# A Fourier filter with a routed FFN on one core: x's loads spread over two queues, part of the score sums on other engines, some first-stage chunks unfolded, and a new plan

## The chip, the cores and the metric

The program runs on one core of a Trainium2 chip, in one launch. Its engines are TensorE (PE, its weight loads PEld), VectorE (DVE), ScalarE (ACT), GpSimd (POOL) and SyncE (SP). Each works through its own list of instructions in order, and they wait for each other by semaphores. DMAs are issued from an engine's queue and run beside the engines. The metric is the device time of one execution in microseconds; a kernel's time is the median of its runs.

## The reference

For each of 8 sequences of 3136 rows by 256 channels, the program filters along the rows in the frequency domain, scores each filtered row, and sends the 128 rows with the highest scores through a gated FFN:

```python
X = np.fft.rfft(x, axis=1)
y = np.fft.irfft(X * (filt_r + 1j * filt_i)[None], n=3136, axis=1)
scores = np.einsum('bsd,d->bs', y, w_gate)
out = y.copy()
for b in range(8):
    top_idx = np.argpartition(-scores[b], 128)[:128]
    xe = y[b, top_idx]
    ye = np.maximum(xe @ w1, 0.0) @ w2
    g = 1.0 / (1.0 + np.exp(-scores[b, top_idx]))
    out[b, top_idx] = xe + g[:, None] * ye
```

All of it is fp32; x and the output are 25.7 MB each.

## The kernel before, in words

The transform of length 3136 is done as 98 times 32. A row index is split as s = 1568 h + 32 a + 16 g + n, and one sequence lies in the tile X as partition 64 g + a (49 rows in the lower half, 49 in the upper), with h, n and the channel along the partition. X is single: the same tile takes the input of a sequence, then the output of an earlier one (there it is called XO), and then the next input.

**Outer stage, inwards** (`outer`, 8 chunks of 32 channels). A chunk is folded: two subtractions or additions of X's halves h (line 347, on DVE or POOL as the table FOLD says), of which one goes to a tile xh and one back into X. Then `amm` (L355) multiplies both by a constant matrix into the PSUM tile pa, of which there is one, and `tout` (L360, a transposing copy on DVE) brings it into the big tile UU.

**Inner stage** (`inner`, 7 groups of four rows of the transform, the last with one). `zmm` (L276) makes pz, ScalarE copies it to q (L280), DVE multiplies pz by one part of the filter into y (L284), GpSimd multiplies q by the other part (L287), and `vmm` (L296) adds both products in the PSUM tile pv, of which there is one. ScalarE copies pv back into UU (L300 to L306); after that DVE multiplies pv by w_gate and sums, once for each of the four rows (`gate`, L312), which gives the scores in the transform's domain. The next `vmm` waits until the last of these has read pv.

**Outer stage, outwards.** `tin` (L339) transposes 32 channels of UU, `ymm` (L401, or three products of split operands L404 to L406 where the table SPLIT says so, whose parts L391 and L395 make) multiplies by the inverse matrix, ScalarE copies the result into X (`yout`, L409). After 8 of the 16 pieces, half of the channels is stored (L424) and the same half of a later sequence is loaded (`load`, L430). In each period the outward stage of sequence t-1, the inner stage of t and the inward stage of t+1 run interleaved.

`select` finds the 128 rows of a sequence by a search over thresholds, `ffn` gathers, multiplies and scatters them. All FFNs stand near the end of the program.

**What sets the order.** Nothing is issued in program order. Every step is recorded by `op(when, engine, cost, ...)`, and a list scheduler at the end of the kernel picks, step by step, the one that its costs say can start first, with due times and leanings from the table PLAN. The lists of all five engines, SP's and ACT's DMA issues among them, are the outcome. The eight semaphores for DMAs from SP and ACT are used in turn, so a DMA that is issued waits for the one eight before it.

**Loads before the change.** Sequences 0 and 1 are loaded with all 256 channels at a time: lower and upper rows in pieces, and the 49th row of each half in DMAs of one partition. From sequence 2 on, a half of the channels (128, rows of 512 bytes) comes in eight DMAs on SP's queue: two for partitions 0 to 47, two for 64 to 111, four for the single partitions 48 and 112. Before the first load, the partitions that pad X are zeroed (`xpad`).

## Time and profile before

| what | us |
|---|---|
| median of 3 runs | 566.62 |
| lowest and highest run | 561.68, 569.27 |
| the profiled execution, by its own time | 570.88 |
| its span, first to last instruction | 569.1 |
| TensorE busy in it | 461.7 (81%) |
| VectorE busy | 412.0 (72%) |
| GpSimd busy | 308.3 (54%) |
| ScalarE busy | 287.2 (50%) |

The profiled execution is 4.3 us above the median of the runs; 1.8 us of it lie outside the span. [...] A busy time of PE counts a matmul in full while it is pipelined with others.

### The profile page before, as it was taken

The page shows a single profiled execution, that of the slowest core. Times are in us where ns is not written, and L with a number is a line of the kernel's source. Part 1 is how long each engine was busy: PE and PEld are TensorE (multiplying, and loading weights), DVE is VectorE, ACT ScalarE, POOL GpSimd, SP SyncE. Part 2 cuts the span into 40 slices and gives each one's busy share as a digit, 9 for nine tenths or more (in the row PEclk, how much of TensorE's full clock was granted, in tenths as well). Part 3 has the DMA queues.
Part 4 walks back from the last instruction along what each step waited for, and adds up shares of the span by engine and source line. Part 5 has one row for each costly group of instructions (what it writes and reads, how often), then busy time and mean ns, then how long its engine had stood idle before and what let it go on. Part 6 is the DMA issues. An engine that isn't in the chain of part 4 may idle for free.

```text
span 569.1 us, 10223 instructions
## 1 busy us (share of the span) xinstructions
PE 461.7 (81%) x3787; PEld 239.2 (42%) x3787; DVE 412.0 (72%) x1050; ACT 287.2 (50%) x573; POOL 308.3 (54%) x203
## 2 busy tenths in 40 slices
PE   4055757798889698799769889989899976999996
PEld 4001324234344243344334334423443554666986
DVE  2065357799969588489758889878899885777442
ACT  1044223056764266256727575657556744777321
POOL 2058667777648651769158549474794555300122
PEclk9555589899999699699989999989999978999989
DMA  9993921970969349861979484959923251075401
GB/s 145 207 241 71 159 32 30 126 90 19 182 115 140 46 123 117 183 82 34 163 158 132 115 114 130 130 142 136 184 25 113 73 186 63 23 218 149 133 28 38
DMA packets 97905, 65.34 MB, mean 115 GB/s; under 512 B 4536, under 2 KB 95800, under 8 KB 97208
## 3 DMA queue, kind: packets, MB, share of 16 engines
q1 hardware_dynamic: 97088, 62.59, 58.3%
q0 software_dynamic: 768, 2.10, 1.1%
q8 instruction: 30, 0.49, 0.4%
q14 instruction: 19, 0.16, 0.1%
HBM read 37.74 MB, written 26.94 MB: 114 GB/s over the span
## 4 chain that ended last, share of the span: by engine, by line
PE 37%; DVE 25%; DMA 20%; POOL 5%; SPq 5%; issue 5%; ACT 3%; POOLq 0%; DVEq 0%; ACTq 0%
DMA X<-in_x_dram 14%; PE pv L296 8%; PE pa L355 7%; DVE rj L312 7%; PE py L401 5%; SPq L430 5%; DVE t L339 4%; DVE UU L360 4%; PE pz L276 3%; DVE y L284 3%; POOL xh L347 3%; PE pv L401 2%; DMA out_dram<-X 2%; DVE xl L395 1%; PE pm L780 1%
## 5 line engine op out<-in xcount | busy, mean ns | idle before, releaser
L287 POOL TENSOR_TENSOR q<-q,fb_sb 128x1024 f32<-128x1024 f32 (+1 forms) x56 | 124.0, 2215 | 86.0 <-ACT q L280 86.0
L355 PE MATMUL pa<-xh,c_sb 49*64 49x512 f32 x256 | 96.6, 702 | 51.8 <-DMA UU<-in_cst_dram 23.5
L347 POOL TENSOR_TENSOR xh<-X 113x512 f32<-113x512 f32 x57 | 73.4, 1292 | 73.7 <-DMA X<-in_x_dram 28.4
L401 PE MATMUL py<-t,c_sb 128*98 128x512 f32 x168 | 95.7, 652 | 9.1 <-ACT X L409 8.9
L360 DVE STREAM_TRANSPOSE UU<-pa 128x1024 f32<-128x1024 f32 x64 | 79.6, 1244 | 28.1 <-PE pa L355 27.6
L312 DVE SCALAR_TENSOR_TENSOR rj<-pv,wg_sb 128x256 bf16<-128x256 f32 x200 | 83.8, 419 | 21.7 <-ACT UU L300 6.1
L339 DVE STREAM_TRANSPOSE t<-UU 128x1024 f32<-128x1024 f32 x64 | 79.0, 1235 | 9.3 <-PE pm L528 7.1
L296 PE MATMUL pv<-y,ti_sb 64*64 64x256 f32 x800 | 73.6, 417 | 13.9 <-DVE rj L312 12.4
L355 PE MATMUL pa<-X,c_sb 49*64 49x512 f32 x256 | 81.5, 708 | 3.6 <-POOL X L347 2.4
L409 ACT COPY X<-py 98x512 f32<-98x512 f32 x96 | 56.0, 584 | 51.4 <-PE py L401 25.6
L276 PE MATMUL pz<-UU,tf_sb 64*64 64x256 f32 x800 | 68.8, 416 | 8.8 <-DVE y L284 5.3
L296 PE MATMUL pv<-q,ti_sb 64*64 64x256 f32 x800 | 71.2, 406 | 5.0 <-POOL q L287 5.0
L280 ACT COPY q<-pz 128x1024 f32<-128x1024 f32 (+1 forms) x56 | 53.1, 948 | 40.6 <-PE pz L276 39.8
L284 DVE TENSOR_TENSOR y<-pz,fa_sb 128x1024 f32<-128x1024 f32 (+1 forms) x56 | 63.6, 1135 | 10.3 <-ACT q L280 10.1
L347 POOL TENSOR_TENSOR X<-X 113x512 f32<-113x512 f32 x49 | 67.2, 1373 | 3.3 <-DVE xh L347 1.6
L355 PEld LDWEIGHTS pa<-xh,c_sb 49*64 49x64 f32 x256 | 19.7, 147 | 90.3 <-DVE xh L347 29.5
L304 ACT COPY UU<-pv 128x1024 f32<-128x1024 f32 x24 | 24.3, 1013 | 53.8 <-PE pv L296 53.7
L276 PEld LDWEIGHTS pz<-UU,tf_sb 64*64 64x64 f32 x800 | 35.2, 143 | 38.3 <-DVE y L284 11.6
L296 PEld LDWEIGHTS pv<-y,ti_sb 64*64 64x64 f32 x800 | 30.9, 142 | 47.3 <-issue 11.7
L296 PEld LDWEIGHTS pv<-q,ti_sb 64*64 64x64 f32 x800 | 35.8, 144 | 20.0 <-POOL q L287 5.9
L401 PEld LDWEIGHTS py<-t,c_sb 128*98 128x98 f32 x168 | 21.5, 168 | 47.5 <-ACT X L409 30.0
L306 ACT COPY UU<-pv 128x1024 f32<-128x1024 f32 x24 | 24.3, 1013 | 27.9 <-PE pv L296 27.2
(209 smaller groups left out, 674.8 us busy)
## 6 DMA issues: line engine op xcount, KB each, us to landing
out_dram<-X SPq DMA_DIRECT2D x16, 1568.0 KB
X<-in_x_dram SPq DMA_DIRECT2D x48, 384.0 KB
R<-scr SPq DMA_DIRECT2D x16, 196.0 KB
X<-in_x_dram SPq DMA_DIRECT2D x4, 768.0 KB
X<-in_x_dram SPq DMA_DIRECT2D x4, 512.0 KB
fb_sb<-in_moe_w_dram SPq DMA_DIRECT2D x2, 1024.0 KB
X<-in_x_dram SPq DMA_DIRECT2D x4, 256.0 KB
fa_sb<-in_fri_dram SPq DMA_DIRECT2D x4, 256.0 KB
```

The costliest lines, as they stand in the source:

```text
L276: nc.tensor.matmul(z[o, hi, e], lhsT=tf_sb[p, l], rhs=urow(b, l, 0, D)[p], start=True, stop=True)
L280: nc.scalar.copy(out=wide(q), in_=wide(h["z"]))
L284: nc.vector.tensor_tensor(out=wide(y), in0=wide(h["z"]), in1=filt(fa_sb), op=ALU.mult)
L287: nc.gpsimd.tensor_tensor(out=wide(h["q"]), in0=wide(h["q"]), in1=filt(fb_sb), op=ALU.mult)
L296: nc.tensor.matmul(v[o, j, c], lhsT=ti_at[p, k, 2 * i + e, hi], rhs=y[p, hi, c], start=k == 0, stop=k == 1)
L312: nc.vector.scalar_tensor_tensor(out=rj, in0=h["v"][:, k % 2, k // 2 * D:k // 2 * D + D], scalar=1.0, in1=wg_sb, op0=ALU.mult, op1=ALU.mul ...
L339: nc.vector.transpose(out=h["t"].rearrange("p d (l j) -> p d l j", j=2), in_=uchan(b_out, c))
L347: eng.tensor_tensor(out=(area(1) if k else h["f"])[:64 + NH], in0=area(0)[:64 + NH], in1=area(1)[:64 + NH], op=(ALU.add, ALU.subtract)[k])
L355: nc.tensor.matmul(ap[64 * k:64 * k + 64, g].rearrange("p (n d) -> p n d", d=DW), lhsT=cc["wa"][p, 64 * k:64 * k + 64], rhs=(area(1) if k ...
L360: nc.vector.transpose(out=uchan(b_in, c), in_=a.rearrange("p (l j) d -> p d l j", j=2))
L401: nc.tensor.matmul(yp[:N1], lhsT=cc["wi"], rhs=half(), start=True, stop=True)
L409: nc.scalar.copy(out=XO[:N1, :, q * CW:(q + 1) * CW], in_=h["y", k][:N1])
```

## The change

Four things change beside the numbers of the plan. **Loads:** every sequence is now loaded by halves of the channels; the upper rows (partitions 64 to 111) are issued from ScalarE's queue, the lower ones and the 49th rows, now both in one DMA of two partitions, from SyncE's. A half has a load key of its own for each of the two groups of rows. **Score sums:** for the groups listed in GPOOL the third and fourth row's gate is no longer read from pv by DVE; GpSimd multiplies UU by w_gate into a tile xl, and ScalarE sums it. **Unfolded chunks:** for those in UNF the two folds fall away and `amm` makes four products in place of two. **Plan:** the costs that the scheduler uses, and all tables and due times, are new. What `select`, `ffn` and the filter compute is unchanged.

```diff
-    FOLD=[[0, 1, 3, 5, 11, 13, 15], [0, 2, 3, 15], [3, 13], [9], [10], [8, 15], [0, 2, 9], [3, 13]],
-    SPLIT=[[5, 7, 11, 12], [], [0], [5, 14], [9, 14], [3, 4, 9], [0, 2, 4, 7, 12, 14], [0, 4, 7, 10, 14]],
...
+    FOLD=[[3, 5, 6, 7, 9, 10, 11, 15], [0, 1, 2, 3, 11, 13, 14, 15], [3, 7, 9, 15], [0, 3, 7, 9, 13], [], [1, 8, 9,
+          13, 14, 15], [2, 7, 9, 13], [0, 1, 2, 3]],
+    SPLIT=[[1], [10, 14], [8, 12, 15], [6, 7, 13, 15], [], [5], [2, 3, 7, 13], [0, 2, 4, 6, 10]],
...
+    UNF=[[2, 3, 7], [1], [], [], [], [], [], []],
+    GPOOL=[[1, 2, 3, 4], [1, 3, 5], [0, 1, 3, 5], [1, 3], [1, 2, 3, 4, 5], [0, 4], [0, 1, 3, 5], [0, 5]],
...
+            def gmul(h=h, i=i):
+                h["g"] = g = hip.tile([128, NG, DW], F32, name="xl", bufs=BUFS["xl"]).rearrange("p a b -> p (a b)").rearrange("p (j d) -> p j d", j=2)
+                r = 2 * i + 1 if b % 2 == 0 else NP - 2 - 2 * i
+                u = UU[:, r, :D] if b % 2 == 0 else UU[:, r, :D, ::-1]
+                nc.gpsimd.tensor_tensor(out=g, in0=u.rearrange("p d j -> p j d"), in1=wg_sb[:, None, :].to_broadcast([128, 2, D]), op=ALU.mult)
+
+            def gsum(h=h, ls=ls):
+                for j in range(2):
+                    rk = sel.tile([128, W_], BF16, name="junk", bufs=1)[:, :D]
+                    nc.scalar.activation(out=rk, in_=h["g"][:, j], func=AF.Copy, accum_out=urow(b, ls[2 + j], D, DS))
...
+                if i in GPOOL[b] and ks == [2, 3]:
+                    G = ("xl", "g", b, i)
+                    op(t0 + 7.2, "pool", 1.3, gmul, [*(u for l in ls[2:] for u in row(b, l)), "wg"], new=G)
+                    op(t0 + 8.5, "act", .9, gsum, [G], [("u", b % 2, l, NDC) for l in ls[2:]])
+                    continue
...
+                wa = [[cc["wa"][:, :64], cc["wa"][:, 64:]], [cc["wa"][:, :64], cc["wn"]]]
+                todo = [[(wa[i][k], area(i)) for i in range(2)] if plainly else [(wa[0][k], area(1) if k else h["f"])] for k in range(2)]
...
-                op(t0 - 1, "pe", .92, amm, [F, *XS, "wa"], new=PA_, mode=1)
+                op(t0 - 1, "pe", 1.83 if plainly else .93, amm, [*XS, "wa"] if plainly else [F, *XS, "wa"], new=PA_, mode=1)
...
-    def rows_in(b, d, parts):
-
-        for g, a, n in parts:
-            for h in range(2):
-                nc.sync.dma_start(out=X[64 * g + a:64 * g + a + n, h, :, d], in_=xv[b, g, a:a + n, h, :, d])
+    def rows_in(b, d, g, eng):
+
+        for h in range(2):
+            eng.dma_start(out=X[64 * g:64 * g + 48, h, :, d], in_=xv[b, g, :48, h, :, d])
+
+    def last_in(b, d):
+
+        for h in range(2):
+            nc.sync.dma_start(out=X[48::64, h, :, d], in_=xv[b, :, 48, h, :, d])
...
+        if b < B:
+            keys = [[("x", h, c, g) for c in range(h * n, h * n + n)] for g in range(2)]
+            op(when, "act", 1.0, lambda: rows_in(b, d, 1, nc.scalar), ["xpad"] if b == 0 else [], keys[1], lat=8.5, bias=bias)
+            op(when + .001, "sp", 6.8, lambda: (rows_in(b, d, 0, nc.sync), last_in(b, d)), ["xpad"] if b == 0 else [], keys[0], lat=2.2, bias=bias)
```

Since the plan is a table of numbers, what it moves is seen in the lists of the engines. In these, a name in brackets is what the instruction waits for: DMAHW0 to DMAHW7 are the eight DMA semaphores in turn, the others engines.

SyncE's list at the start of the program. X is the input tile, fa_sb and fb_sb are parts of the filter, ti_sb and tf_sb the matrices of the inner stage, wg_sb is w_gate, c_sb holds the constant matrices. Before:

```order
L430 DMA X<-in_x_dram 48x4096 x2
L430 DMA X<-in_x_dram 32x4096 x2
L919 DMA c_sb<-in_cst_dram 128x128
L874 DMA fa_sb<-in_fri_dram 32x1024 x2
L874 DMA fb_sb<-in_fri_dram 32x1024
L874 DMA fb_sb<-in_fri_dram 32x1024 [waits DMAHW0_49]
L430 DMA X<-in_x_dram 16x4096 [waits DMAHW1_49,DVE_49]
L430 DMA X<-in_x_dram 16x4096 [waits DMAHW2_49,Pool_49]
L430 DMA X<-in_x_dram 1x4096 [waits DMAHW3_49]
```

and with the change:

```order
L977 DMA ti_sb<-in_ti_dram 128x1664
L900 DMA fa_sb<-in_fri_dram 32x1024 x2
L900 DMA fb_sb<-in_fri_dram 32x1024 x2
L945 DMA c_sb<-in_cst_dram 128x192
L950 DMA tf_sb<-in_tf_dram 128x1600
L951 DMA wg_sb<-in_moe_w_gate_dram 128x256
L454 DMA X<-in_x_dram 48x16x128 [waits DMAHW0_49,DVE_49]
L454 DMA X<-in_x_dram 48x16x128 [waits DMAHW2_49,Pool_49]
L459 DMA X<-in_x_dram 2x16x128 [waits DMAHW4_49]
```

Eight table loads now stand ahead of x, x comes by half its channels, and the single rows of 4096 elements (four DMAs of one partition before) come with each half in DMAs of two partitions.

GpSimd's list in the inner stage of sequence 0, with the folds (xh, X) of sequence 1 among it. Before:

```order
L287 TENSOR_TENSOR q<-q,fb_sb 128x1024 [waits DMAHW6_49,Activation_49]
L287 TENSOR_TENSOR q<-q,fb_sb 128x1024 [waits Activation_49]
L347 TENSOR_TENSOR xh<-X 113x512 [waits DMAHW4_49,DMAHW3_49,DMAHW5_49,DMAHW2_49,DMAHW6_49,DMAHW1_49,DMAHW7_49,DMAHW0_49,DVE_49]
L347 TENSOR_TENSOR X<-X 113x16x32 [waits DVE_49]
L287 TENSOR_TENSOR q<-q,fb_sb 128x1024 [waits Activation_49]
```

and with the change, from the second product q on:

```order
L292 TENSOR_TENSOR q<-q,fb_sb 128x1024 [waits Activation_49]
L369 TENSOR_TENSOR X<-X 113x16x32 [waits Pool_49]
L369 TENSOR_TENSOR xh<-X 113x512 [waits DMAHW3_49,DMAHW2_49,DMAHW4_49,DMAHW1_49,DMAHW5_49,DMAHW0_49,PE_49]
L292 TENSOR_TENSOR q<-q,fb_sb 128x1024 [waits Activation_49]
L369 TENSOR_TENSOR X<-X 113x16x32 [waits Pool_49]
L292 TENSOR_TENSOR q<-q,fb_sb 128x1024 [waits Activation_49]
L331 TENSOR_TENSOR xl<-UU,wg_sb 128x512 [waits DVE_49]
```

Before, three of the seven products q stand ahead of the fold that waits for all of sequence 1; now two stand ahead of the fold that waits for its second half, and products for the scores (xl) stand among the q.

The first load that follows a store, that of the first half of sequence 3. Before, all of it is on SyncE's list, behind the store:

```order
L424 DMA out_dram<-X 3136x1x128 [waits DMAHW5_49,Activation_49,Pool_49]
L430 DMA X<-in_x_dram 48x16x128 [waits DMAHW6_49,DMAHW5_49]
L430 DMA X<-in_x_dram 48x16x128 [waits DMAHW7_49,PE_49]
L430 DMA X<-in_x_dram 48x16x128 [waits DMAHW0_49]
L430 DMA X<-in_x_dram 48x16x128 [waits DMAHW1_49,PE_49]
L430 DMA X<-in_x_dram 1x16x128
```

With the change, ScalarE's list at that place holds the upper rows between its other work:

```order
L545 ACTIVATE junk,cnt<-R,nb 128x392 [waits Activation_49]
L311 COPY UU<-pv 128x2x512 [waits PE_49]
L434 COPY X<-py 98x32x16 [waits PE_49]
L568 ACTIVATE ok,J<-pm,c_sb 128x15 [waits PE_49]
L569 ACTIVATE nb<-J,nd 128x1 [waits DVE_49,Activation_49]
L454 DMA X<-in_x_dram 48x16x128 [waits DMAHW5_49,DMAHW2_49]
L454 DMA X<-in_x_dram 48x16x128
L434 COPY X<-py 98x32x16 [waits PE_49]
```

DMAHW5 is there the landing of the store: ScalarE's list now stops at it until the half is stored, as SyncE's does.

## Rows read from the trace of the kernel before

**Rows 1.** The head of the page: the span with its count of instructions, and the busy time of each engine, its share of the span and its instructions.

```profile
span 569.1 us, 10223 instructions
PE 461.7 (81%) x3787; PEld 239.2 (42%) x3787; DVE 412.0 (72%) x1050; ACT 287.2 (50%) x573; POOL 308.3 (54%) x203
```

**Rows 2.** The page's chain of work that ended last, as shares of the span by engine.

```profile
PE 37%; DVE 25%; DMA 20%; POOL 5%; SPq 5%; issue 5%; ACT 3%; POOLq 0%; DVEq 0%; ACTq 0%
```

**Rows 3.** The chain of waits in order of time, the stretch from the start to 79 us: start in us, duration in us, what. `x8` counts merged instructions.

```profile
1.66 15.02 DMA X<-in_x_dram
16.73 9.48 DMA X<-in_x_dram
26.23 4.61 DMA UU<-in_cst_dram
...
34.64 1.26 DVE UU L360
36.04 2.04 PE pa L355 x8
...
56.81 2.02 PE pa L355 x8
58.84 8.63 DMA X<-in_x_dram
67.49 11.36 DMA X<-in_x_dram
```

**Rows 4.** The chain of waits again, asked for 28 to 120 us, one turn of the inner loop of sequence 0.

```profile
90.50 1.99 PE pv L296 x32
...
92.52 1.02 ACT UU L304
...
93.57 0.45 DVE rj L312 x2
...
95.55 1.96 PE pv L296 x32
```

**Rows 5.** GpSimd in order of time, 72 to 84 us: start in us, duration in us, engine, line, operation, out<-in, shapes, and in brackets the engine's idle time before it with what ended it.

```profile
72.44 2.36 POOL L287 TENSOR_TENSOR q<-q,fb_sb 128x1024 f32<-128x1024 f32 x1 [2.41 <-ACT q L280]
79.06 1.69 POOL L347 TENSOR_TENSOR xh<-X 113x512 f32<-113x512 f32 x1 [4.27 <-DMA X<-in_x_dram]
...
81.93 2.35 POOL L287 TENSOR_TENSOR q<-q,fb_sb 128x1024 f32<-128x1024 f32 x1
```

**Rows 6.** SyncE's DMA issues in order of time, same columns; the duration is that of issuing, `x8` counts the DMAs that were issued one behind the other.

```profile
0.74 1.89 SPq L430 DMA_DIRECT2D X<-in_x_dram  x4
...
140.42 0.99 SPq L424 DMA_DIRECT2D out_dram<-X  x1
148.97 7.56 SPq L430 DMA_DIRECT2D X<-in_x_dram  x8
```

**Rows 7.** The chain of waits over the whole span, five of its pieces after 150 us that are a landing of x.

```profile
155.94 7.53 DMA X<-in_x_dram
...
181.87 7.93 DMA X<-in_x_dram
...
282.83 7.96 DMA X<-in_x_dram
...
308.26 7.22 DMA X<-in_x_dram
...
364.45 5.98 DMA X<-in_x_dram
```

**Rows 8.** What the DMA engines moved in single stretches (in the order in which they were asked for): stretch in us, its length, busy us and count of instructions of PE, PEld, DVE, ACT and POOL, granted TensorE clock, then the busy share of the DMA engines and their GB/s.

```profile
154.00:156.00 2.00, 2.00 (x30) 1.00 (x22) 2.00 (x5) 1.52 (x4) 1.92 (x2) 1.00 1.23 132
156.00:157.00 1.00, 0.85 (x7) 0.20 (x6) 1.00 (x1) 0.52 (x1) 0.38 (x1) 1.00 1.25 165
157.00:159.00 2.00, 1.50 (x10) 0.52 (x4) 1.90 (x11) 1.13 (x4) 0.00 (x0) 1.00 1.23 132
...
28.00:30.00 2.00, 0.00 (x0) 0.00 (x0) 0.00 (x0) 0.00 (x0) 0.00 (x0) 0.50 0.96 361
38.00:44.00 6.00, 3.04 (x19) 0.67 (x16) 5.67 (x5) 5.95 (x4) 5.62 (x4) 0.50 1.01 248
4.00:12.00 8.00, 3.31 (x43) 3.17 (x41) 1.13 (x1) 0.00 (x0) 0.50 (x1) 1.00 1.00 135
166.00:172.00 6.00, 5.74 (x67) 3.28 (x65) 4.22 (x9) 2.72 (x7) 6.00 (x5) 1.00 0.82 231
```

**Rows 9.** The same columns for two stages: the inward outer stage of sequence 0 alone, and the middle of the program.

```profile
30.00:59.00 29.00, 17.67 (x64) 3.04 (x64) 19.56 (x19) 13.59 (x8) 21.50 (x13) 0.50 0.64 143
...
140.00:450.00 310.00, 272.41 (x2319) 119.78 (x2311) 254.04 (x666) 181.54 (x393) 191.26 (x122) 0.95 0.67 118
```

**Rows 10.** Groups of instructions by line, engine, operation, tile and shape: count, busy us in all and mean ns of one, idle us of the engine just before them and what ended it.

```profile
L312 DVE SCALAR_TENSOR_TENSOR rj<-pv,wg_sb 128x256 bf16<-128x256 f32 x200 | 83.8, 419 | 21.7 <-ACT UU L300 6.1 <-ACT UU L304 5.6 <-ACT UU L306 5.6
...
L347 POOL TENSOR_TENSOR xh<-X 113x512 f32<-113x512 f32 x57 | 73.4, 1292 | 73.7 <-DMA X<-in_x_dram 28.4 <-PE pa L355 18.2 <-DMA wg_sb<-in_moe_w_gate_dram 8.1
...
L312 DVE DVE_READ_ACCUMULATOR rj<-pv,wg_sb 128x1 f32 x200 | 16.5, 82 | 0.0
...
L519 ACT ACTIVATION_READ_ACCUMULATOR junk<-R,nb 128x1 fp32r x48 | 9.0, 188 | 0.0
...
L300 ACT COPY UU<-pv 128x256 f32<-128x256 f32 x8 | 3.1, 385 | 5.7 <-PE pv L296 5.7
```

More of the change, by code (lines that the diff above doesn't have):

```diff
@@ L315, in inner @@
             parts = sorted({part_of[2 * i + e] for e in range(m)})
-            op(t0, "pe", .46 * m + .02, zmm, [u for l in ls for u in row(b, l)] + ["tf"], new=Z, mode=1)
+            op(t0, "pe", .49 * m + .02, zmm, [u for l in ls for u in row(b, l)] + ["tf"], new=Z, mode=1)
             op(t0 + 1.0, "act", .15 + .43 * m, zout, [Z], [Z], new=Q)
-            op(t0 + 1.0, "dve", .12 + .52 * m, pmul, [Z, *(("fa", k) for k in parts)], new=Y)
-            op(t0 + 2.0, "pool", 1.25 * m, qmul, [Q, *(("fb", k) for k in parts)], [Q])
+            op(t0 + 1.0, "dve", .12 + .54 * m, pmul, [Z, *(("fa", k) for k in parts)], new=Y)
@@ L320, in inner @@
+            op(t0 + 2.0, "pool", 1.2 * m, qmul, [Q, *(("fb", k) for k in parts)], [Q])
             op(t0 + 4.5, "pe", .88 * m + .02, vmm, [Y, Q, "ti"], new=V, mode=1)
             op(t0 + 6.2, "act", .15 + .43 * m if n > 1 else .3, vout, [V], [V, *(u for l in ls for u in row(b, l))])
+            def gmul(h=h, i=i):
[3 more added lines that the diff above has]
+                nc.gpsimd.tensor_tensor(out=g, in0=u.rearrange("p d j -> p j d"), in1=wg_sb[:, None, :].to_broadcast([128, 2, D]), op=ALU.mult)
@@ L333, in outer @@
             hx = c * DW // HD
-            XS = [("x", hx, 2 * c), ("x", hx, 2 * c + 1)]
+            plainly = b_in < B and c in UNF[b_in]
+            XS = [("x", hx, 2 * c, g) for g in range(2)] + [("x", hx, 2 * c + 1, g) for g in range(2)]
             def tin(h=h, c=c):
@@ L348, in fold, with amm @@
                                   op=(ALU.add, ALU.subtract)[k])
-            def amm(h=h, area=area):
+            def amm(h=h, area=area, plainly=plainly):
                 h["a"] = ap = ps_a.tile([128, 2, 512], F32, name="pa")
-                for g in range(2):
-                    for k in range(2):
-                        p = slice(64 * g, 64 * g + NH)
-                        nc.tensor.matmul(ap[64 * k:64 * k + 64, g].rearrange("p (n d) -> p n d", d=DW),
-                                         lhsT=cc["wa"][p, 64 * k:64 * k + 64], rhs=(area(1) if k else h["f"])[p], start=True, stop=True)
+                wa = [[cc["wa"][:, :64], cc["wa"][:, 64:]], [cc["wa"][:, :64], cc["wn"]]]
+                todo = [[(wa[i][k], area(i)) for i in range(2)] if plainly else [(wa[0][k], area(1) if k else h["f"])] for k in range(2)]
+                for i in range(len(todo[0])):
+                    for g in range(2):
+                        for k in range(2):
+                            p = slice(64 * g, 64 * g + NH)
+                            nc.tensor.matmul(ap[64 * k:64 * k + 64, g].rearrange("p (n d) -> p n d", d=DW),
+                                             lhsT=todo[k][i][0][p], rhs=todo[k][i][1][p], start=i == 0, stop=i == len(todo[k]) - 1)
             def tout(h=h, c=c):
@@ L883, in consts @@
     def consts():
-        nc.sync.dma_start(out=c_sb[:, 128:], in_=cst[:, NCUT + 128:])
+        nc.sync.dma_start(out=c_sb[:, 192:], in_=cst[:, NCUT + 192:])
     raw = stage
@@ L918 @@
         op(-99.5, "pe", .2 * WARM, warmup, (), (), new=("m", "warm"))
[L919 removed]
+    op(-99, "sp", .3, lambda: nc.sync.dma_start(out=c_sb[:, :192], in_=cst[:, NCUT:NCUT + 192]), (), ["wa"], lat=2)
     for k, e in ((0, "dve"), (1, "pool")):
@@ L956 @@
     for h in range(2):
-        load(TS + TC0 * NCH + 1 + .1 * h, 1, h, xys[1], XA)
+        load(TS + TC0 * NCH / 2 * (h + 1) + 1, 1, h, xys[1], XA)
     for t in range(B + 1):
```

68 lines of the change are left out of this document (31 added, 37 removed).

## The prediction, made before the changed kernel had run

> **What bounds the kernel now.** I read the page's head first: TensorE is busy 461.7 of 569.1 us, no other engine over 72% [rows 1], so what PE waits for is what can be won. The chain of waits says what that is: DMA holds 20% of it, more than GpSimd and ScalarE together [rows 2]. Read in order of time, it begins with x. To 30.84 us it is loads alone, and the first matmul of the outer stage starts there. Then matmuls and transposing copies alternate: 2.04 us of PE, 1.26 of DVE, one turn per chunk, because pa is single. The last of the eight chunks ends at 58.83, and the next 20 us are again a load, that of sequence 1, all 256 channels at once [rows 3]. GpSimd stands at it: its third product q ended at 74.80, the fold behind it could start at 79.06 only, and the fourth product came at 81.93 [rows 5]. The inner stage then runs by a turn of 5.05 us: vmm 1.99, ScalarE's copy 1.02, four sums of about 0.46, next vmm [rows 4].
>
> In the middle of the program PE is busy 272.4 of 310 us, DVE 254.0 [rows 9]. The 37.6 us that PE idles there go with x again: five landings of 6 to 8 us are on the chain [rows 7]. Each belongs to a load that follows its store; the store was issued at 140.42, the first DMA of the load at 148.97 [rows 6], and the load landed at 155.94 + 7.53 = 163.47 [rows 7]. So a half (3136 rows of 512 bytes, 1.61 MB) takes 14.5 us, behind a store of 8.5.
>
> Why so long is in the transfer rates [rows 8]. While one group of 48 partitions is written, x moves at 132 GB/s, and at 135 at the start, where its pieces are 16 KB; so it is not the size of the pieces. A store of the same 512-byte rows ran at 231, tables over all 128 partitions at 361, and filter parts that alternate between lower and upper 32 partitions at 248. Inside the load, at 156 to 157 us, where the engines cross from the lower to the upper partitions and both are written, the rate rose to 165 and fell back to 132. The partitions written bound the load.
>
> **The change, part by part**, against the profiled execution's 570.9 us.
>
> *The load.* With ScalarE's queue, both groups of partitions are written at once. No row shows that in full. Bounds: 132 GB/s (nothing won) and 264 (twice). I take 240, between the store's 231 and the 248 of the alternating tables. 1.61 MB then takes 6.7 us in place of 12.2; with the 2.3 us that the old load had besides (14.5 less 12.2), 9.0 us. [...]
>
> *The start.* Eight tables go ahead of x: 1.90 MB over all partitions at 361 GB/s is 5.3 us, 0.52 MB of filter at 248 is 2.1 [rows 8]; begun at 1.7, they are through at 9.1. The first half of x lands 9.0 us later, at 18.1, and the first chunk is an unfolded one, so PE starts there and not at 30.85. At 14.5 us a load it would be 23.6. The outer stage took 28.0 us; three unfolded chunks add a second set of products, 3 x 2.04 = 6.1 us at the granted clock of 0.50, its lower level [rows 3, 9], so it ends at 52.2, not 58.83: **-6.6**. If the higher level is granted there, each product halves and some 6 us more are won.
>
> *Sequence 1's load.* Its first half can start when four chunks (two of them unfolded) are through, at 18.1 + 14.0 + 4.1 = 36.2, and lands at 45.2, before it is wanted. The second lands 9 us after 52.2, at 61, where GpSimd is through with two products; before, three of them ended 16 us after the outer stage. I take the 79 us stall as gone. Its price: GpSimd idled 4.3 us, and the fourth product came 7.1 us after the third had ended [rows 5], while vmm and folds queued behind. I take **-7**, between 4.3 and 10.
>
> *Gates.* For 26 of the 56 groups two sums leave DVE. Where the inner stage runs alone, the turn shortens by two of them, 0.93 us [rows 4]; four such groups in sequence 0: **-3.7**. The other 22 free DVE of 44 x (0.419 + 0.082) = 22 us [rows 10]. DVE has a quarter of the chain [rows 2], so some 5; I take **-4**. What replaces them: 26 products on GpSimd of about 1.29 us (nearest row: the fold of 512 elements), 34 us, while 19 fewer folds there save 25; 52 sums on ScalarE of 0.385 + 0.188 = 0.57, 30 us [rows 10]. GpSimd idles 46%, ScalarE 50% [rows 1]; I cost both at nothing. Without that cover (third rival) it is up to 30. DVE's eleven more folds lie beside PE, as their waits did before.
>
> *The middle.* Five loads on the chain, 5.5 us shorter each: 27.5 at most. When they leave, PE at 88% and DVE at 82% are late next, so I keep half: **-14**, bounds 0 and -27.5.
>
> *ScalarE's new wait.* Ten times its list now stops until a store has landed, up to 8.5 us after the half's last copy [rows 6]. Queued behind are copies of pz, pv and py, for which GpSimd and PE wait. In the new list 7 to 17 other instructions stand between the half's last copy and the load; at 287.2 / 573 = 0.50 us each [rows 1] that is 3.5 to 8.5 us of work even if ScalarE never waited. The stalls sum to at most 21 us, and since ScalarE is half idle I take 0.
>
> *The end* (from 450 us, PE full of FFN) I leave: 0, within 6 either way.
>
> Sum: -6.6 - 7 - 3.7 - 4 - 14 = -35.3, so 535.6 for a profiled execution. The one of before is 4.3 above its median of 566.6; the forecast for the median is **531**.
>
> [...]
>
> **The rivals.**
> 1. *Two queues, one rate.* The load stays at 14.5. For it: the DMA engines are already marked busy all the time (shares over 1.2); against it, the 165 and 248 GB/s [rows 8]. Then x lands at 23.6 and the outer stage ends at 57.7 (-1.1), sequence 1's second half at 72.2, so of the stall 4 is won, the gates stay (-7.7), the middle gives 0: -12.8, **554**. Also so if ScalarE comes late to its half, and the change does not do what it says.
> 2. *The two queues hinder each other* (the other side). If alternating between them makes a half land 20 us after its issue, the lists, in which folds and products queue behind x on GpSimd and DVE, stall at each: five on the chain give +27.5, the start and sequence 1 about +11, less the 8 of the gates: **597**. It decides from a landing of about 18 us on. For it only that no row shows two queues; against it rows 8.
> 3. *Cover gone.* ScalarE's stops (21) and its 30 us of sums slow the copies; the start's 17 are won, the middle loses 11: **561**. For it: products q waited for ScalarE's copy of pz already [rows 5].
>
> **How the numbers follow.** Forecast 0.57, rival 1 0.20, rival 3 0.11, rival 2 0.06, and 0.06 for more than the forecast's upper bounds (the higher clock at the start, all 27.5 of the middle: 510 or so). The likeliest is 531. The range 512 to 557 takes in rival 1 and both ends of the middle; it leaves out rival 2, most of 3 and the far end. About 2% (11 us) can be told from no change, so faster means below 555: the forecast, the far end and more than half of rival 1, 0.77; same 0.16; slower 0.07.
>
> **What would show it.** Right: first outer matmul near 18 us; x at over 200 GB/s with both groups in flight; first DMA to landing about 9 us; no wait for x on GpSimd in sequence 0; a period of the stores some 3 us shorter. Wrong: 130 GB/s and 14 us again (rival 1); ScalarE idle before its x DMAs, with GpSimd waiting for q behind it (rival 3); landings over 18 us (rival 2). If the loads are at 9 us and the time is still above 545, the step that failed is the half that I keep in the middle.

## The result, and the profile of the changed kernel

The changed kernel took **529.9 us** in the median (529.0 to 532.5 in four runs), against 567.0 for the kernel before in the same study: a ratio of 0.937, 95% interval 0.929 to 0.944. The forecast was 531, in a range of 512 to 557. The time came out, by luck: the way to it did not, as the experiments show. Times of experiments below are medians of undisturbed executions, since some executions (among them the profiled one of e1, which is therefore not split by stretches) were disturbed and ran some per cent longer.

The head of the changed kernel's page, and its chain of waits by engine; they answer to [rows 1, 2].

```profile
span 530.7 us, 10315 instructions
...
PE 450.9 (85%) x3816; PEld 226.8 (43%) x3816; DVE 406.3 (77%) x956; ACT 309.0 (58%) x674; POOL 317.5 (60%) x208
...
PE 40%; DMA 33%; DVE 10%; ACT 7%; POOL 5%; issue 4%; POOLq 0%; ACTq 0%; DVEq 0%; SPq 0%
```

DVE's share of the chain fell from 25% to 10%, that of DMA rose from 20% to 33%. Of the latter the page gives 20% to the loads of x; before, it gave them 14% and their issuing on SyncE's queue (SPq) another 5%, so x bounds both kernels about alike. Most of the rest are the filter's parts at the start (6%, none of it on the chain before) and the scratch memory of `select` (5%). Where the time went is seen by cutting the span at two events that both kernels have: the issue of the first store, and that of the store of sequence 5's first half. The stretches of the kernel before (columns as in [rows 8]):

```profile
0.00:140.42 140.42, 86.63 (x761) 39.68 (x765) 82.69 (x141) 45.36 (x53) 83.84 (x56) 0.74 0.64 113
140.42:425.87 285.45, 249.27 (x2120) 109.89 (x2116) 232.30 (x597) 165.13 (x359) 177.65 (x114) 0.95 0.71 122
425.87:569.10 143.23, 125.79 (x918) 89.67 (x910) 97.05 (x314) 76.67 (x161) 46.84 (x35) 0.95 0.34 102
```

and of the changed one:

```profile
0.00:125.90 125.90, 87.69 (x823) 38.30 (x827) 85.21 (x130) 53.12 (x85) 81.78 (x54) 0.80 0.70 126
125.90:400.45 274.55, 243.66 (x2109) 105.46 (x2101) 230.97 (x540) 178.54 (x425) 183.88 (x117) 0.95 0.71 127
400.45:530.70 130.25, 119.53 (x889) 83.01 (x889) 90.11 (x289) 77.37 (x167) 51.81 (x39) 0.98 0.38 112
```

The start won 14.5 us (forecast 17.3), the middle 10.9 (forecast 18), and the end, which I had left at 0, 13.0.

**The start.** TensorE in order of time, the first chunk's products and the last products of sequence 0's outer stage:

```profile
19.75 1.98 PE L380 MATMUL pa<-X,c_sb 49*64 49x512 f32 x8 [13.27 <-DMA X<-in_x_dram]
22.95 2.24 PE L380 MATMUL pa<-X,c_sb 49*64 49x512 f32 x8 [1.21 <-DMA X<-in_x_dram]
...
50.45 3.69 PE L380 MATMUL pa<-X,c_sb 49*64 49x512 f32 x16 [1.39 <-DVE UU L385]
```

It began at 19.75 (forecast 18.1) and ended at 54.14 (forecast 52.2; 58.83 before). But the forecast let it begin on a whole load: it began with the rows of X's half h = 0 alone, and those of h = 1 kept it waiting until 22.95. The last of this load landed at 23.2, 17.1 us after its first DMA (6.11). TensorE's granted clock, as a share of full speed, stands at 0.50 or 1.00 in the traces of both kernels, and a mean over a stretch lies between; from 17 to 59 us it was 0.50, as the sum had it. In the kernel before, a chunk's eight products that took 2.04 us there took 0.95 at 1.00 (at 97.50 us). Behind the outer stage, where the load of sequence 1 stood before, TensorE was busy for 16.5 of the 20 us from 59 to 79 at a clock of 0.93, against 11.5 at 0.71 before, and from 79 to 109 the clock was 1.00 against 0.87; no term of the sum had that. GpSimd in order of time, with the fold of sequence 1 and the first products q:

```profile
54.78 1.77 POOL L369 TENSOR_TENSOR xh<-X 113x512 f32<-113x512 f32 x1 [4.55 <-DMA X<-in_x_dram]
...
63.26 2.38 POOL L292 TENSOR_TENSOR q<-q,fb_sb 128x1024 f32<-128x1024 f32 x1 [2.85 <-ACT q L285]
...
66.83 2.37 POOL L292 TENSOR_TENSOR q<-q,fb_sb 128x1024 f32<-128x1024 f32 x1
...
73.41 2.40 POOL L292 TENSOR_TENSOR q<-q,fb_sb 128x1024 f32<-128x1024 f32 x1
```

The stall of [rows 5], which stood between the third and the fourth product, is gone; GpSimd now waits 4.55 us for sequence 1 ahead of all products, and the first of them then still waits for ScalarE. The chain of waits up to sequence 1's landing:

```profile
25.78 9.65 DMA fa_sb<-in_fri_dram
...
35.45 9.59 DMA fb_sb<-in_fri_dram
...
45.06 10.79 DMA fa_sb<-in_fri_dram
...
55.91 11.39 DMA X<-in_x_dram
```

Parts of the filter go through the same queue, and the sum had priced only those ahead of the first load. The first half of sequence 1 was issued at 36.86, as forecast (36.2), but landed at 54.4 and not at 45.2; the second landed at 67.3 and not at 61.

**A load behind its store.** SyncE in order of time, the first store and the load behind it:

```profile
125.90 0.97 SPq L449 DMA_DIRECT2D out_dram<-X  x1
134.91 0.90 SPq L454 DMA_DIRECT2D X<-in_x_dram  x2
135.84 1.65 SPq L459 DMA_DIRECT2D X<-in_x_dram  x2
```

ScalarE's part of it, and its landing on the chain of waits:

```profile
135.55 0.95 ACTq L454 DMA_DIRECT2D X<-in_x_dram  x2
```

```profile
135.89 12.54 DMA X<-in_x_dram
```

From 134.91 to 135.89 + 12.54 = 148.43 it took 13.5 us, not 9.0. The transfer rates in it (columns as in [rows 8]) show why:

```profile
139.00:141.00 2.00, 2.00 (x20) 0.93 (x19) 0.72 (x4) 1.85 (x6) 0.00 (x0) 1.00 1.23 120
141.00:143.00 2.00, 1.44 (x5) 0.41 (x3) 1.61 (x2) 1.76 (x6) 1.46 (x1) 1.00 1.22 189
143.00:145.00 2.00, 1.33 (x25) 0.84 (x28) 1.79 (x7) 0.59 (x1) 0.91 (x1) 1.00 1.26 132
```

ScalarE came 0.6 us after SyncE, behind both of its DMAs, and the queues were served in the order of issue: SyncE's two large DMAs had landed by 144.1 us, ScalarE's at 146.2 and 148.4, with 120 and 132 GB/s while one group of partitions was written, 189 only where the engines crossed from one to the other. A landing is read from the last increment of the DMAs' semaphores in the trace. By that the ten loads behind stores took 14.0 us in the mean (11.3 to 15.3), against 14.8 before; ScalarE came 0.2 to 4.9 us late, and once 1.4 us early. Only the two loads of sequence 2, which no store precedes and where both engines issued at the same moment, took 10.7 and 10.9.

The same holds for all seven kernels of this study that load from two queues (this one, e3, e3b, e4, e5, e7, e8), 70 loads behind stores. In 22 of them the two engines issued within 0.25 us of each other, and they took 10.7 to 12.2 us. In 46 ScalarE came 0.64 to 5.6 us later or 0.5 to 1.6 us earlier, and they took 12.9 to 16.6. Two at 0.57 and 0.60 us took 11.7 and 11.4.

### The profile page after: what moved, and what is told of

It is laid out like the page before. It is cut to its first block, busy times and chain, and to the rows that moved or that the text cites. A ratio compares the mean times of both kernels' runs of the same rounds, so it can differ in the third digit from the quotient of the medians.

```text
span 530.7 us, 10315 instructions
## 1 busy us (share of the span) xinstructions
PE 450.9 (85%) x3816; PEld 226.8 (43%) x3816; DVE 406.3 (77%) x956; ACT 309.0 (58%) x674; POOL 317.5 (60%) x208
## 4 chain that ended last, share of the span: by engine, by line
PE 40%; DMA 33%; DVE 10%; ACT 7%; POOL 5%; issue 4%; POOLq 0%; ACTq 0%; DVEq 0%; SPq 0%
DMA X<-in_x_dram 20%; PE pv L301 9%; PE py L426 9%; PE pa L380 6%; DVE X L369 4%; DMA fa_sb<-in_fri_dram 4%; PE pz L281 3%; DMA scr<-kf 3%; PE pa L426 2%; DVE UU L385 2%; POOL xh L369 2%; DMA fb_sb<-in_fri_dram 2%; DMA R<-scr 2%; PE pa L839 2%; POOL X L369 2%
## 5 line engine op out<-in xcount | busy, mean ns | idle before, releaser
L426 PE MATMUL py<-t,c_sb 128*98 128x512 f32 x190 | 105.6, 638 | 10.7 <-ACT X L434 10.2
L369 POOL TENSOR_TENSOR xh<-X 113x512 f32<-113x512 f32 x51 | 68.0, 1338 | 77.1 <-DMA X<-in_x_dram 33.4
L380 PE MATMUL pa<-X,c_sb 49*64 49x512 f32 x304 | 86.5, 755 | 25.1 <-DMA X<-in_x_dram 14.5
L380 PE MATMUL pa<-xh,c_sb 49*64 49x512 f32 x240 | 81.5, 664 | 17.8 <-DVE UU L385 10.2
L434 ACT COPY X<-py 98x512 f32<-98x512 f32 x112 | 65.7, 586 | 40.0 <-PE py L426 15.5
L317 DVE SCALAR_TENSOR_TENSOR rj<-pv,wg_sb 128x256 bf16<-128x256 f32 x148 | 62.0, 419 | 16.0 <-ACT UU L311 7.0
L281 PE MATMUL pz<-UU,tf_sb 64*64 64x256 f32 x800 | 61.5, 406 | 7.6 <-DVE y L289 7.3
L369 POOL TENSOR_TENSOR X<-X 113x512 f32<-113x512 f32 x36 | 48.4, 1345 | 1.1
L301 PEld LDWEIGHTS pv<-y,ti_sb 64*64 64x64 f32 x800 | 30.1, 137 | 41.5 <-issue 11.5
L281 PEld LDWEIGHTS pz<-UU,tf_sb 64*64 64x64 f32 x800 | 29.7, 136 | 41.7 <-DVE y L289 11.1
L331 POOL TENSOR_TENSOR xl<-UU,wg_sb 128x512 f32<-128x512 f32 x26 | 35.8, 1378 | 19.1 <-ACT UU L311 10.5
L301 PEld LDWEIGHTS pv<-q,ti_sb 64*64 64x64 f32 x800 | 34.7, 138 | 13.6 <-issue 2.2
L369 DVE TENSOR_TENSOR X<-X 113x512 f32<-113x512 f32 x24 | 33.8, 1408 | 6.7 <-POOL xh L369 6.6
```

Of the source, the lines that this page charges most:

```text
L281: nc.tensor.matmul(z[o, hi, e], lhsT=tf_sb[p, l], rhs=urow(b, l, 0, D)[p], start=True, stop=True)
L301: nc.tensor.matmul(v[o, j, c], lhsT=ti_at[p, k, 2 * i + e, hi], rhs=y[p, hi, c], start=k == 0, stop=k == 1)
L317: nc.vector.scalar_tensor_tensor(out=rj, in0=h["v"][:, k % 2, k // 2 * D:k // 2 * D + D], scalar=1.0, in1=wg_sb, op0=ALU.mult, op1=ALU.mul ...
L369: eng.tensor_tensor(out=(area(1) if k else h["f"])[:64 + NH], in0=area(0)[:64 + NH], in1=area(1)[:64 + NH], op=(ALU.add, ALU.subtract)[k])
L380: nc.tensor.matmul(ap[64 * k:64 * k + 64, g].rearrange("p (n d) -> p n d", d=DW), lhsT=todo[k][i][0][p], rhs=todo[k][i][1][p], start=i == ...
L426: nc.tensor.matmul(yp[:N1], lhsT=cc["wi"], rhs=half(), start=True, stop=True)
```

## The experiments

All but m1 and e10 are the changed kernel with one thing altered; in e5 and e7 that thing is a set of numbers of the plan. Each is split at the same two events; "load" is the mean of the ten loads behind stores. Stretches and loads are those of the one profiled execution, so they need not add up to the median (for e8 they add up to 553.0). The interval of e3, e3b is that of e3b.

| kernel | median | ratio to before, 95% interval | start | middle | end | load |
|---|---|---|---|---|---|---|
| before | 567.0 | | 140.4 | 285.5 | 143.2 | 14.8 |
| changed | 529.9 | 0.929 to 0.944 | 125.9 | 274.6 | 130.3 | 14.0 |
| e1 one queue, lower first | 534.5 | 0.937 to 0.949 | | | | 14.6 |
| e2 one queue, in turn | 524.7 | 0.918 to 0.934 | 124.4 | 270.5 | 130.9 | 13.7 |
| e9 the same, 8 half-size DMAs | 512.1 | 0.897 to 0.908 | 120.3 | 259.6 | 130.9 | 11.8 |
| e11 8 half-size, no turns | 535.4 | 0.937 to 0.948 | 128.0 | 276.0 | 129.7 | 14.0 |
| e8 ScalarE earlier | 560.2 | 0.985 to 0.995 | 125.9 | 295.8 | 131.3 | 12.9 |
| e3, e3b sums on VectorE | 540.9 | 0.950 to 0.960 | 131.1 | 273.2 | 132.0 | 13.8 |
| e4 folded | 536.5 | 0.937 to 0.955 | 128.9 | 274.0 | 131.7 | 13.3 |
| e7 old end | 541.5 | 0.950 to 0.963 | 125.8 | 272.7 | 142.1 | 13.6 |
| e5 old plan, new loads | 552.7 | 0.962 to 0.979 | 136.0 | 269.5 | 145.9 | 12.0 |
| e10 before, in turn | 560.0 | 0.975 to 0.991 | 139.0 | 275.0 | 145.0 | 13.5 |

### The loads by themselves (m1)

```python
one_by_one:  rows(SP, 0, 0); rows(SP, 0, 1); rows(SP, 1, 0); rows(SP, 1, 1)   # partition group, half h
two_queues:  rows(ACT, 1, h), rows(SP, 0, h) for both h, issued at the same moment
alternating: rows(SP, 0, 0); rows(SP, 1, 0); rows(SP, 0, 1); rows(SP, 1, 1)
fine:        the same in 8 DMAs of 8 rows each
fine_two:    the same 8 DMAs, the upper ones from ACT, the lower ones from SP
```

> This kernel leaves out the whole computation. It loads halves of x into X, ten forms one after the other, twice, with a DVE memset between two forms that waits for all of the one before. The forms: the 48 lower then the 48 upper partitions from SyncE's queue (as before the change); upper from ScalarE's and lower from SyncE's at the same moment (as the change means it); SyncE alone with lower and upper DMAs in turn; two queues with ScalarE 2 us late; SyncE alone and two queues with DMAs of half the size in turn; only the lower partitions (half the bytes) from one queue and from two; the 49th rows as two DMAs of two partitions and as four of one. Theory 'partitions' (a load is bound by the partitions written, so it is fast where lower and upper DMAs are in flight together, from whatever queue): one after the other about 12.5 us for 1.57 MB (two stretches of 6 us at 132 GB/s), two queues at the same moment 7 to 9 us, in turn on one queue 8 to 11, ScalarE 2 us late 9 to 11, lower only 6.5 from either. Theory 'queues' (two queues give what one cannot, the order is all one): two queues 7 to 9, in turn on one queue 12.5 as before, lower only from two queues faster than from one. Theory 'nothing won' (the first rival of the prediction): all full forms 12 to 13. [...]

DVE in order of time; each memset waits for the whole form before it, in brackets how long. Forms in order: one by one, two queues, alternating; then "fine" between 61.47 and 72.48; the last two are the 49th rows as two DMAs of two partitions and as four of one.

```profile
24.96 0.07 DVE L36 MEMSET X<- 128x16 f32 x1 [13.26 <-DMA X<-in_x_dram]
...
36.24 0.07 DVE L36 MEMSET X<- 128x16 f32 x1 [11.18 <-DMA X<-in_x_dram]
...
49.28 0.07 DVE L36 MEMSET X<- 128x16 f32 x1 [12.94 <-DMA X<-in_x_dram]
...
61.47 0.07 DVE L37 MEMSET X<- 128x16 f32 x1
...
72.48 0.07 DVE L37 MEMSET X<- 128x16 f32 x1 [1.76 <-DMA X<-in_x_dram]
...
98.92 0.07 DVE L36 MEMSET X<- 128x16 f32 x1 [3.11 <-DMA X<-in_x_dram]
...
103.28 0.07 DVE L36 MEMSET X<- 128x16 f32 x1 [4.25 <-DMA X<-in_x_dram]
```

Issue to landing, first and second round: one by one 13.1 and 13.3, two queues 11.0 and 10.7, in turn on one queue 12.75 and 11.8, fine on one queue 10.8 and 10.6, fine on two queues 9.5 and 9.1 (its first two DMAs went out while the form before it was still landing). The lower partitions alone (half the bytes) took 7.7 and 7.8 from one queue and 7.2 and 7.3 from two. So 9.0 us, the forecast's load, is not reached by the form that the change uses even with nothing beside it: between 28 and 34 us its rate was 238, 153 and 200 GB/s in turn, where the forecast had 240 throughout. Short turns over both queues come near, and no kernel here has them. A second queue helps where it brings the other partitions (13.2 to 10.9 us), and hardly where it brings the same (7.7 and 7.8 to 7.2 and 7.3); and turns on one queue do as much as two queues with large DMAs if they are short (10.7 and 10.9). That refutes both pure theories: the order counts, the number of queues counts less. The form in which ScalarE was meant to come 2 us late took 10.5, because it wasn't late: its DMAs went out 0.12 us after the copy ahead of them had begun. One rival is left in all of this: the lower partitions take other rows of x (the first 16 of every 32) than the upper ones, so the rows read change with the partitions written, and no run tells which of the two asks for the turns. What in the hardware makes the order count, no run shows.

### One queue again, in two orders (e1, e2)

```diff
# e1
-op(when, "act", 1.0, lambda: rows_in(b, d, 1, nc.scalar), ...)
+op(when, "act", 1.0, lambda: None, ...)
-lambda: (rows_in(b, d, 0, nc.sync), last_in(b, d))
+lambda: (rows_in(b, d, 0, nc.sync), rows_in(b, d, 1, nc.sync), last_in(b, d))
# e2: as e1, but
+for h in range(2):
+    for g in range(2):
+        nc.sync.dma_start(out=X[64 * g:64 * g + 48, h, :, d], in_=xv[b, g, :48, h, :, d])
```

> The changed kernel with the upper rows issued from SyncE's queue again, lower before upper as before the change; ScalarE's place in the plan stays and issues nothing, the lists of TensorE, VectorE and GpSimd are those of the changed kernel. Theory 'the second queue': what the loads won is the second queue; sequence 2's two loads go from 10.7 to about 14.5 us, the others lose the 0.8 us that they had won, and the first load is 3 to 5 us later: 540 to 545 us. Theory 'the plan': loads behind stores were no shorter with two queues (14.0 against 14.8 us), the gain is that of the plan and of the sums: 529 to 534. Theory 'ScalarE's stop' (its list no longer waits for the stores): below 527.

> The changed kernel with all rows of x on SyncE's queue, lower and upper DMAs in turn (lower, upper, lower, upper, then the 49th rows); ScalarE's place in the plan issues nothing, the lists of TensorE, VectorE and GpSimd are those of the changed kernel. By the bare loads (13.1 and 13.3 us one after the other, 12.75 and 11.8 in turn on one queue, 11.0 and 10.7 on two queues) a load takes 0.3 to 1.5 us less than with lower before upper on one queue, whose kernel took 534.7. Theory 'two queues at the same moment' (the order is worth little, what counts is that two queues hold work): 532 to 535. Theory 'order' (it is the turns between lower and upper partitions that count): 527 to 531, as good as the changed kernel or better, since ScalarE doesn't stop for the stores.

e1 took 534.5, just above the range of "the plan" and well short of that of "the second queue"; e2 took 524.7, even less than "order" had. So the second queue, in this plan and with ScalarE's stops for the stores counted in, is worth 4.6 us, and the plain order of the same four DMAs on one queue twice that (9.8). e2 is faster than the changed kernel, though its loads are only 0.3 us shorter; what of the 5.2 us is ScalarE's freedom from the stores was not tried.

### Shorter turns, and small DMAs without turns (e9, e11)

```diff
# e9: order (h, n, g); e11: order (g, h, n)
+for n in range(0, NG, NG // 2):
+    nc.sync.dma_start(out=X[64 * g:64 * g + 48, h, n:n + NG // 2, d], in_=xv[b, g, :48, h, n:n + NG // 2, d])
```

> The changed kernel with all rows of x on SyncE's queue as in the kernel with turns, but eight DMAs of half the size in turn in place of four: the lower and the upper partitions take turns every 8 of the 16 rows. The bare loads took 10.8 and 10.6 us so, 12.75 and 11.8 with four in turn, and the kernel with four in turn took 526.1. Theory 'the turns count': loads behind stores of 11 to 12.5 us in place of 13.7, 518 to 524. Theory 'issue' (six more issues a load of 0.4 to 0.6 us, with the waits for the eight semaphores, hold up SyncE's queue and the small DMAs of select behind it): 526 to 532 with loads no shorter.

> The kernel with eight DMAs of half the size on SyncE's queue, without the turns: the four of the lower partitions first, then the four of the upper ones, then the 49th rows. With eight in turn it took 512.1 us and loads behind stores took 11.8; with four large ones, lower first, 534.7 and 14.6. Theory 'the turns count' (the rate is that of the partitions being written, small DMAs alone change nothing): loads of 14 to 15 us, 531 to 537. Theory 'small DMAs count' (the queue overlaps several of them, whichever partitions they write): loads of 11.5 to 12.5 us, 511 to 517. In between, each has a part.

e9 took **512.1 us**, the best of the study, faster than both kernels and 6 us below the range of "the turns count", though its loads of 11.8 lie in that theory's range. e11, with the same DMAs in the other order, took 535.4, as e1. Without turns the smaller size wins nothing; with them it wins 12.6 us (e2 to e9). The three stretches of e9, and the middle one of e11:

```profile
0.00:120.33 120.33, 89.47 (x823) 42.25 (x827) 85.17 (x130) 52.95 (x85) 80.45 (x54) 0.80 0.64 132
120.33:379.91 259.58, 236.49 (x2091) 103.71 (x2087) 230.44 (x537) 178.64 (x424) 183.82 (x117) 0.97 0.66 134
379.91:510.80 130.89, 120.63 (x914) 83.69 (x906) 91.49 (x291) 77.30 (x167) 51.81 (x39) 0.98 0.38 111
```

```profile
127.97:403.93 275.96, 245.55 (x2091) 106.65 (x2087) 229.69 (x537) 179.34 (x424) 184.16 (x117) 0.94 0.72 126
```

SyncE's issues of e9, the second load behind a store, and GpSimd's wait for it, which is still 3.6 us:

```profile
152.09 3.92 SPq L461 DMA_DIRECT2D X<-in_x_dram  x8
156.06 1.60 SPq L466 DMA_DIRECT2D X<-in_x_dram  x2
```

```profile
164.59 2.55 POOL L369 TENSOR_TENSOR xh<-X 113x512 f32<-113x512 f32 x2 [3.61 <-DMA X<-in_x_dram]
```

In the load before it, the shortest of the ten (10.0 us), x moved at 193 to 225 GB/s:

```profile
130.00:132.00 2.00, 2.00 (x14) 0.63 (x14) 1.26 (x3) 1.40 (x4) 0.47 (x1) 1.00 0.98 225
132.00:134.00 2.00, 2.00 (x17) 0.89 (x17) 1.86 (x6) 1.59 (x7) 0.00 (x0) 1.00 1.19 193
134.00:136.00 2.00, 1.90 (x20) 0.77 (x12) 0.32 (x2) 1.97 (x6) 0.03 (x1) 1.00 1.22 208
```

The pair also gives the price of a load. Ten loads, 2.2 us shorter each, are 22 us; the middle of e9 is 16.4 us shorter than e11's. So three quarters of what the ten loads lose comes back. From e2 to e9 it is 10.9 of 19, from before to e5 16 of 28, from before to e10 10.4 of 13: more than half in every pair.

Less than half of the 16.4 us is waiting. The middle has the same 2091 products in both; TensorE's idle time in it is 23.1 us in e9 and 30.4 in e11, which makes 7.3 us, and the other 9.1 are busy time, at a granted clock of 0.97 in e9 and 0.94 in e11 (over the whole span 0.936 to 0.943 in the four executions of e9, 0.912 to 0.926 in those of e11). In e11 the first load behind a store landed at 150.0 us; the stretches around that:

```profile
148.00:152.00 4.00, 1.89 (x19) 0.59 (x11) 1.84 (x3) 2.26 (x6) 1.82 (x2) 1.00 0.26 28
152.00:156.00 4.00, 3.98 (x25) 1.48 (x29) 3.96 (x7) 1.81 (x4) 4.00 (x3) 0.61 0.87 225
156.00:160.00 4.00, 4.00 (x37) 2.48 (x31) 3.67 (x9) 1.02 (x4) 4.00 (x3) 0.53 0.93 270
```

TensorE stood for 2.1 us of the first one, and then worked for 8 us at a clock of 0.61 and 0.53. So this landing was paid twice, as idle time and as slower products behind it.

### ScalarE's part earlier in its list (e8)

```diff
+steps = []
+for n in order:
...
+    at, left = len(steps), 4
+    while left and not (prog[steps[at - 1]][2] == "sp" and ("out" in ...)):
+        at -= 1
...
+        left -= prog[steps[at]][2] == "act"
+    steps.insert(at, n)
+order = steps
```

(`order` is the scheduler's list; n is a load of ScalarE, and "out" is the key that a store writes.)

> The changed kernel with ScalarE's part of the ten loads that follow a store four steps earlier in its list, but never ahead of the store's issue; nothing else moves. In the changed kernel ScalarE issued 0.6 to 5 us behind SyncE in most of them, and they took 14.0 us in the mean; with the old plan both issued together and they took 11.5. Theory 'ScalarE's lateness is what the load lost': loads of 11 to 12.5 us and 3 to 8 us less in all, 522 to 527. Theory 'cover' (ScalarE's stop for the store costs as much as the load wins): 528 to 533 with shorter loads. Theory 'stop dearer': above 534.

560.2 us: "stop dearer", by 30 us (in the profiled execution, the fastest, by 22, of which 21 are in the middle). Where both issued together the loads took 10.7 to 11.7, as hoped; in four, ScalarE came first by 1.5 us and they took 15 to 16.6. ScalarE in order of time before one of the loads:

```profile
160.94 0.59 ACT L435 COPY X<-py 98x512 f32<-98x512 f32 x1
164.38 1.02 ACTq L455 DMA_DIRECT2D X<-in_x_dram  x2
165.50 0.62 ACT L552 ACTIVATE junk<-R,nb 128x392 bf16<-128x392 f32 x1 [3.97 <-issue]
```

It did no work for 4 us, until the store had landed. TensorE's waits for ScalarE's copies into X, in e8 (us in total, times, longest):

```profile
PE py L427 <- ACT X L435: 25.4, 18, 5.2
```

and in the changed kernel:

```profile
PE py L426 <- ACT X L434: 10.2, 15, 1.1
```

TensorE's granted clock from 130 to 400 us fell with that, from 0.95 to 0.91. How the 30 us divide into waits, clock and the four longer loads no run shows.

### The sums, the unfolded chunks, the end of the plan (e3, e3b, e4, e7)

```diff
# e3, e3b
-op(t0 + 7.2, "pool", 1.3, gmul, ...);  op(t0 + 8.5, "act", .9, gsum, ...)
+op(t0 + 7.2, "pool", 1.3, lambda: None, ...);  op(t0 + 8.5, "act", .9, lambda: None, ...)
+# at the place of the first two sums: gate([0, 1, 2, 3])
```

> The changed kernel with all four score sums on VectorE again, read from pv, at the place where the plan has the first two; GpSimd's products with w_gate and ScalarE's sums are left out of their lists, the other lists are the same. Theory 'price of the prediction' (gates -7.7 in all): 537 to 539. Theory 'sums carry the middle and the end' (in the last inner stage of before, VectorE's four sums are the chain; the end won 13 us that the prediction had at 0): 545 to 560. Theory 'no worth' (ScalarE and GpSimd lose as much as VectorE wins): 526 to 532.

> The kernel with all four sums on VectorE once more, for an interval: its undisturbed runs were 538.0 and 540.9 us. Theory 'price of the prediction': 537 to 539. Theory 'dearer than that': 539 to 543.

Seven executions, 537.9 to 543.8, median 540.9: the sums are worth some 11 us, where I had 7.7. TensorE waits for VectorE's sums again, about as often as before the change (13 times, 12.4 us); in the changed kernel it does so twice, for 1.1 us in all. In e3:

```profile
PE pv L301 <- DVE rj L317: 11.6, 14, 2.2
```

The profiled execution, 538.0, is one of the fastest: in it the start is 5.2 us longer, middle and end together by 0.3. Where the rest lies in the longer ones is not shown.

```diff
# e4, in amm
+if plainly:
+    for k in range(2):   # both folds on VectorE, into xr and X
+        nc.vector.tensor_tensor(...)
+plainly = False
```

> The changed kernel with the four unfolded chunks folded again: at the place where TensorE's products stand, VectorE makes both folds, and TensorE two products in place of four; the rest of the lists is the same. The prediction charged the second set of products in sequence 0 with 6.1 us. Theory 'charged rightly, folds hidden': 524 to 527. Theory 'the folds are as dear' (two on VectorE, 0.75 and 1.2 us, ahead of the products, against 2.04 saved per chunk): 528 to 532. Theory 'unfolding is a gain' (VectorE and the single pa are the chain there): 533 to 538.

536.5 us; its executions (533.1 to 537.5) lie above all four of the changed kernel. Unfolding four chunks is a gain, some 6 us, though it doubles their products; in the profiled executions, which are 3.8 us apart, 3.0 of it lie at the start. The first products then wait for x alone, not for folds behind x: they begin at 19.75, with folds at 23.32.

```diff
# e7, in PLAN
-P7=38.237, ... S7=58.481, FL=-66.93, ... LAST=['y', 'a', 'y', 'a'], TRING=['z', 'v'], URING=['m', 'v', 'm', 'v']
+P7=62.431, ... S7=1.894, FL=13.835, ... LAST=['a', 'v'], TRING=['m', 'z', 'v'], URING=['m', 'z', 'm', 'v']
```

> The changed kernel with the end of the old plan: the due times of the last select, of the last outer stages and of the FFNs, the rings LAST, TRING and URING (which PSUM tiles the last outer stages and the FFNs take) and WPOOL are those of before. The lists are those of the changed kernel up to the inner stage of the last sequence, after which they differ. From the first store of sequence 5 to the end it took 143.2 us before, 145.9 with the new loads under the old plan, 130.3 with the change, 132.0 with the sums on VectorE again. Theory 'the plan's end' (the 13 us of the end are those numbers, above all that the last outer stages no longer take pv): 540 to 545. Theory 'the state in which the end is reached' (what the earlier part leaves to the end): 528 to 533.

541.5 us, with the end at 142.1: 11.8 of the 13 us of the end are the plan's. Some 8 of these 11.8 are idle time of TensorE, and 5.1 of it lie where the inner stage of sequence 7 runs; the stretch in e7 and in the changed kernel:

```profile
430.00:462.00 32.00, 25.16 (x225) 17.74 (x218) 22.14 (x73) 20.08 (x38) 16.46 (x12) 0.94 0.27 89
```

```profile
430.00:462.00 32.00, 30.29 (x257) 18.29 (x250) 26.41 (x85) 25.96 (x55) 17.61 (x13) 1.00 0.64 192
```

With the old end, outer products of the last sequences go to pv, which the inner stage needs too (the tile's instructions in e7, first and last start):

```profile
L426 PE MATMUL pv<-t,c_sb x26: 591/592/651, 415.7 to 489.9; 128*98 128x512 f32 x26
```

The last vmm of the inner stage began at 454.1; on the chain one of these outer products stands at 415.9, the next at 465.5. With the new rings they use py and pa, and TensorE is busy for 30.3 of the 32 us, not 25.2. Rings and due times were changed together; which of the two counts for more was not tried.

### The old plan with the new loads, and the old kernel with turns (e5, e10)

```diff
# e5: PLAN of before, UNF and GPOOL empty, in the changed code
# e10: kernel before
-for g, a, n in parts:
-    for h in range(2):
+for h in range(2):
+    for g, a, n in parts:
```

> The changed kernel with the plan of before in place of the new one, and without sums on GpSimd and unfolded chunks: what is left of the change is the loads by halves over two queues, with slightly other costs in the scheduler. The plan's numbers were not chosen for these loads, so a loss of some us may come with that. Theory 'the loads' : the start and the landings of x win 15 us or more also under the old plan: 545 to 555. Theory 'the plan': 560 to 575, since the loads behind stores are hardly shorter.

> The kernel before the change with one thing altered: the two loops over x's DMAs are swapped, so that lower and upper partitions take turns on SyncE's queue; the order of all other instructions on all engines is that of before. In the changed kernel the same turns were worth 8 us (534.7 with the lower ones first, 526.1). Theory 'the turns count' (a load is some 1 us shorter, five landings are on the chain, and the first load and sequence 1's are on it too): 555 to 562. Theory 'only with the new plan' (before, other waits stand behind the landings): 564 to 568.

e5 took 552.7. In the old plan ScalarE is at its part of the load together with SyncE in eight of ten; the loads took 12.0 in the mean (median 11.5, the figure in e8's expectation), and the middle won 16 us. So the two queues can bring both groups together, at 11.5 us a load and not at 9; the change's own plan mostly doesn't let them. e10, one swapped pair of loops, won some 7 us: its loads took 13.5, and its middle is 10.4 shorter. Theory "the turns count" holds also without the new plan.

## Why the prediction was right, and where it was not

**The total** was right by luck, because three errors offset each other: 2.8 us too much at the start, 7.1 too much in the middle, 13.0 too little at the end.

**The load, 9.0 us: the step that failed.** It rested on 240 GB/s for both groups at once and on their being in flight together. Bare, with both queues at the same moment, it is 10.9, since the rate swung between 153 and 238 GB/s; in the kernel 14.0, since ScalarE comes late and the queues are then served one after the other, at 120 and 132 GB/s. That is the first rival ("two queues, one rate"), in the form "also so if ScalarE comes late to its half"; its time, 554, is wrong only because of what follows.

**The middle, -14 and -4.** The half that I kept was too small, not too large: more than half of ten loads came back, three quarters in the cleanest pair (e9 against e11), where I had counted half of five. The clock is part of that, and the sum had no term for it. With 0.8 us won per load, 8 in all, that makes 6 of the 10.9 us at most; the sums show nothing there in the profiled execution of e3, so the remaining 5 fall, by elimination, to the new lists, which no run took apart.

**The end, 0 within 6: mis-sized.** It was -13, and it is the plan's end (e7: 11.8 of it). I had read [rows 9] up to 450 us only and taken TensorE for full after that. The trace of before has it idle for 143.2 - 125.8 = 17.4 us in that stretch, above; of the 13.0 us won, 6.7 are less idle time and 6.3 less busy time.

**The start.** The outer stage of sequence 0: -4.7 for -6.6, its first products 1.65 us late. Gates in sequence 0: -5.2 (e3) for -3.7. Together it is -14.5 for -17.3, which leaves -4.6 for the stall of sequence 1, forecast at -7 between 4.3 and 10: it is gone, but its loads landed 9 and 6 us later than forecast.

**ScalarE's new wait, 0 with at most 21.** 0 was about right for this plan, in which ScalarE turns to its load when the store has already landed; that is the reason for its lateness. The 5.2 us of e2, where ScalarE never stops and the loads are hardly shorter, leave room for a few. The upper bound was too low for another order: four steps earlier it costs 30. Cover (third rival) is not gone where the plan leaves 7 to 17 instructions ahead, and is gone with up to four fewer.

**The 49th rows.** The sum had no term for their new form, which I had thought the dearer. Bare, two DMAs of two partitions took 3.1 to 3.3 us and four of one 4.1 to 4.3: they are 1 us cheaper.
